# Query weights loaded and used ahead of the down weights, and 256 KB of the down weights dealt to 48 and 16 partitions, in a one-core decode step

## The chip, the core and the metric

The kernel runs on one core of a Trainium2 chip. A core has TensorE (PE; its weight loads are shown as PEld), VectorE (DVE), ScalarE (ACT), GpSimd (POOL), SyncE (SP, which here issues almost all transfers), and sixteen DMA engines that move data between HBM and the core's memory. The metric is the device time of one execution in microseconds (us); less is better. Before the change the median of three runs is 199.74 us (199.58 to 199.85).

## The reference

One decode step of a block: sliding-window attention over a cache, gated by a gated linear unit, for a batch of 8 rows and one new token each (D = 512).

```python
x = A_x                                    # [8, 1, 512] bf16
xn = _layernorm(x, axis=-1)
# A: 32 query heads, 8 K/V heads, head size 128, the last W = 2048 of 8192 cache rows
q = (xn @ wq) ...                          # wq [512, 4096]
scores = einsum("bhqd,bhkd->bhqk", q, k) * 128 ** -0.5
o = einsum("bhqk,bhkd->bhqd", softmax(scores), v)
s = o.reshape(8, 1, 4096) @ wo             # wo [4096, 512]
# B: F = 1792
h = sigmoid(xn @ w_gate) * (xn @ w_up)     # [512, 1792] each
g = silu(h @ w_down)                       # w_down [1792, 512]
return x + s * g
```

All inputs are bf16. The K and V windows are 33.5 MB each, the weights 14 MB.

## The kernel before, in words

**Transfers.** SP issues them in an order written out as a list, `todo`. `later` (L107) appends a tile's load with its pool's name; `pump` (L110) issues from the head of the list as long as the pool of the head has `room` (5 tiles of 16 KB per partition for "k", 4 for "v"); `free` (L116) gives a place back at the point of the program where a tile has been used, and pumps again. The instruction then waits on the chip until the place is really free. The order on SP's queue is the order of the list:

1. `x_bf` and the second half of the gate weights (L149, L151); ACT's queue loads the first half and `x4_sb` (L157)
2. `wu_sb`, the up weights, all rows
3. `wd_sb`, the down weights (L194): of the 14 rows of 512 that each of 128 partitions owns, rows 1 to 13
4. `wq_sb`, the query weights, in two tiles of 2 MB (L196)
5. `wd_part` (`want_part`, L179): the 128 rows left over, one per partition as `wd_sb` counts, dealt into another tile
6. sixteen K tiles and sixteen V tiles of 2 MB each (L202, L204), and `wo_sb` in five pieces (L206)

**The dealt rows.** `wd_part` is a tile of 64 partitions by 3 rows, cleared by a POOL memset (L183), and filled by three transfers (`PARTS`, L175 and L176): 20 partitions by 3 rows, again 20 by 3, and 8 by 1. `p0, n` are the partitions, `s0` the first of the rows, and `a` (5, 5, 4) is the outermost count on the HBM side; the inner piece is one row of 1 KB. Since rows in `wd_part` sit in other partitions than the values of the hidden layer that multiply them, three small matmuls (L327) with selection matrices `sel_part` (L276 to L285, a memset and seven DVE copies out of an identity) bring those values there, and a DVE copy makes `hP_sb` (L335).

**The first stage.** PE runs its instructions in program order: the gate and up products (`hidden`, L291), `hP_ps`, the 16 down products `w_ps` (L348: 13 from `wd_sb`, 3 from `wd_part`), the regrouping `b_ps` (L361), then the 32 query products `q_ps` (L385) and their transposes (L404), and then the attention, which starts with transposes of K (L481). ACT and DVE copy between (`w_sb` L358, `sigb` L371, `gg_sb` L375, `q_bf` L399 and L401, `qm_sb` L407).

**The attention.** For each of 8 batch rows two K tiles are transposed in parts of 8 (L481, DVE copies L486), multiplied with the queries (`scores`, L493), and two rows later in the loop the V tiles are multiplied (`values`, L591). PE, DVE and ACT interleave three batch rows. A used K or V tile calls `free`, which issues the next load.

**The end.** The output weights come in rows 0 to 12, 12 to 20, 20 to 26, 26 to 30 and 30 to 32. The first twenty products go to `part_ps` (L719), the last twelve to `fin_ps` (L733), each as its piece lands; then `prod` (L748), `y_bf` (L750) and the output transfer (L751).

Of the kernel before, what the change touches and what calls it, by code (L numbers as in the profile page):

```python
# [10 lines left out]
def kernel(  # L11
# [13 lines left out]
    nc = tc.nc  # L25
    P = 128
    B, _, D = A_x.shape
    _, Hkv, Sk, Dh = A_k_cache.shape
# [5 lines left out]
    FT = F // P  # L34
# [14 lines left out]
    bf16 = mybir.dt.bfloat16  # L49
    f32 = mybir.dt.float32  # L50
    AF = mybir.ActivationFunctionType
    ALU = mybir.AluOpType
# [6 lines left out]
    vpool = ctx.enter_context(tc.tile_pool(name="vpool", bufs=4))  # L59
    ktpool = ctx.enter_context(tc.tile_pool(name="ktpool", bufs=3))  # L60
    ppool = ctx.enter_context(tc.tile_pool(name="ppool", bufs=2))
    consts = ctx.enter_context(tc.tile_pool(name="consts", bufs=1))
    work = ctx.enter_context(tc.tile_pool(name="work", bufs=1))
    small = ctx.enter_context(tc.tile_pool(name="small", bufs=2))
    ps_t = ctx.enter_context(
        tc.tile_pool(name="ps_t", bufs=4, space=bass.MemoryType.PSUM)
    )
    ps_s = ctx.enter_context(
        tc.tile_pool(name="ps_s", bufs=2, space=bass.MemoryType.PSUM)
    )  # L70
# [3 lines left out]
    ps_m = ctx.enter_context(  # L74
        tc.tile_pool(name="ps_m", bufs=1, space=bass.MemoryType.PSUM)
    )
    ctx.enter_context(tc.manual_schedule())


# [1 line left out]
    q0, q1 = nc.sync, nc.scalar  # L81
    k_tiles = {}
    v_tiles = {}
    room = {"k": 5, "v": 4}
    pools = {"k": kpool, "v": vpool}

    def load_cache(cache, tag, b, i):
# [16 lines left out]
    weights = {}  # L104
    todo = []

    def later(tag, f):  # L107
        todo.append((tag, f))
# [7 lines left out]
    def free(tag):  # L116
        room[tag] += 1
        pump()

    def want_rows(name, w, tag, per, r0, r1):  # L120
        def f():
            t = load_rows(w, tag, per, r0, r1, name)
            for r in range(r0, r1):
                weights[(name, r)] = t[:, r - r0, :]

        later(tag, f)
# [13 lines left out]
    Z = 32  # L140
    S = Z // B
    NB = D // P
# [24 lines left out]

    A = 5  # L170
    SD = 1
    SX = 3
    HP = P // 2
    NA = 4 * A
    PARTS = ((0, NA, 0, SX, 0, A), (Z, NA, 0, SX, SX * NA, A))  # L175
    PARTS += ((Z + NA, P - 2 * SX * NA, 0, 1, 2 * SX * NA, 4),)  # L176
    d_room = []

    def want_part(w, per):  # L179
        def f():  # L180
            d = vpool.tile([HP, SX, SD, w.shape[1]], bf16, name="wd_part", tag="v")
            d_room.append(d)
            nc.gpsimd.memset(d[:], 0.0)  # L183
            for p0, n, x0, x1, s0, a in PARTS:
                m = n * (x1 - x0)
                src = w.rearrange("(y r) n -> y (r n)", r=per)[s0 : s0 + m]
                q0.dma_start(
                    out=d[p0 : p0 + n, x0:x1].rearrange("p x r n -> p (x r n)"),
                    in_=src.rearrange("(y a) n -> a y n", a=a)[:, :, : SD * w.shape[1]],
                )  # L190

        later("v", f)

    want_rows("wd_sb", B_w_down, "v", FT, SD, FT)  # L194
    for i in range(2):
        want_rows("wq_sb", A_wq, "k", KT, 2 * i, 2 * i + 2)  # L196
    want_part(B_w_down, FT)
    order = [(b, i) for b in range(B) for i in range(NQ)]
    AHEAD = 3
# [5 lines left out]
    for t0, t1 in ((0, 12), (12, KS), (KS, 26), (26, 30), (30, RT)):  # L205
# [4 lines left out]
    ident = consts.tile([P, P], bf16, name="ident")  # L210
# [6 lines left out]
        out=perm[:].rearrange("k (l p) -> k l p", l=G),  # L217
        in_=ident[:].rearrange("k (p l) -> k l p", l=G),
# [13 lines left out]
        out=rstd[:], in_=mv[:, 1:2], func=AF.Sqrt, bias=eps_t[:], scale=1.0  # L232
# [4 lines left out]
        out=xn_bf[:],  # L237
        in0=x_f[:],
# [7 lines left out]
    for kt in range(KT):  # L246
        nc.tensor.transpose(  # L247
            out=xnT_ps[:, kt, :],
            in_=xn_bf[:].rearrange("b (p kt) -> b kt p", kt=KT)[:, kt, :],
# [11 lines left out]
    for t in p_buf:  # L261
        nc.vector.memzero(t[:])
    oP_sb = work.tile([P, RT, Z], bf16, name="oP_sb")
    nc.vector.memzero(oP_sb[:])

    NDQ = Dh // RT
    own_q = consts.tile([P, NDQ], f32, name="own_q")
    nc.vector.reduce_sum(
        out=own_q[:], in_=ident_f[:].rearrange("k (h q) -> k q h", q=NDQ), axis=AX.X
    )  # L270
    sel_z = consts.tile([P, Z], f32, name="sel_z")
    nc.vector.reduce_sum(
        out=sel_z[:], in_=ident_f[:].rearrange("k (j z) -> k z j", z=Z), axis=AX.X
    )

    sel_part = consts.tile([P, SX, HP], bf16, name="sel_part")  # L276
    nc.vector.memzero(sel_part[:])
    for p0, n, x0, x1, s0, a in PARTS:
        for x in range(x0, x1):
            nc.vector.tensor_copy(  # L280
                out=sel_part[:, x, p0 : p0 + n].rearrange("k (a e) -> k a e", a=a),
                in_=ident[:, s0 : s0 + n * (x1 - x0)].rearrange(
                    "k (e x a) -> k x a e", x=x1 - x0, a=a
                )[:, x - x0],
            )  # L285

    FC = F // NB

    def hidden(name):  # L291
# [21 lines left out]
        out=h_sb[:].rearrange("k t p -> k p t"),  # L313
        in0=sig[:, :FC].rearrange("k (p t) -> k p t", t=FT),
        in1=u_ps[:].rearrange("k (p t) -> k p t", t=FT),
        op=ALU.mult,
    )
    free("v")
    hT_sb = work.tile([P, FT, Z], bf16, name="hT_sb")
    nc.vector.transpose(  # L320
        out=hT_sb[:].rearrange("k t z -> k (t z)"),
        in_=h_sb[:].rearrange("k t p -> k (t p)"),
    )

    hP_ps = ps_t.tile([HP, SX, SD * Z], f32, name="hP_ps", tag="t")
    for x in range(SX):
        nc.tensor.matmul(  # L327
            hP_ps[:, x, :],
            lhsT=sel_part[:, x, :],
            rhs=hT_sb[:, :SD, :].rearrange("p t z -> p (t z)"),  # L330
            start=True,
            stop=True,
        )
    hP_sb = work.tile([HP, SX, SD * Z], bf16, name="hP_sb")
    nc.vector.tensor_copy(out=hP_sb[:], in_=hP_ps[:])  # L335
    down = [(hT_sb[:, t, :], weights[("wd_sb", t)]) for t in range(SD, FT)]
    for x in range(SX):
        top = max(p0 + n for p0, n, x0, x1, _, _ in PARTS if x0 <= x < x1)
        down += [
            (hP_sb[:top, x, Z * r : Z * (r + 1)], d_room[0][:top, x, r, :])  # L340
            for r in range(SD)
        ]


    w_ps = ps_s.tile([P, D], f32, name="w_ps", tag="s")
    for t, (h, w) in enumerate(down):
        j = t % NB
        nc.tensor.matmul(  # L348
            w_ps[Z * j : Z * (j + 1), :],
            lhsT=h,  # L350
            rhs=w,
            start=(t < NB),
            stop=(t >= len(down) - NB),
            tile_position=(0, Z * j),
            skip_group_check=True,
        )
    w_sb = ktpool.tile([P, 2, 512], f32, name="w_sb", tag="kT")
    nc.scalar.copy(out=w_sb[:, 0], in_=w_ps[:])  # L358
    b_ps = ps_s.tile([P, P], f32, name="b_ps", tag="s")
    for j in range(NB):  # L360
        nc.tensor.matmul(  # L361
            b_ps[Z * j : Z * (j + 1), :],
            lhsT=sel_z[:],
            rhs=w_sb[:, 0, j * P : (j + 1) * P],
            start=True,
            stop=True,
            tile_position=(0, Z * j),
            skip_group_check=True,
        )
    sigb = work.tile([P, P], f32, name="sigb")  # L370
    nc.scalar.activation(out=sigb[:], in_=b_ps[:], func=AF.Sigmoid)  # L371
    free("v")
    free("v")
    gg_sb = work.tile([P, P], f32, name="gg_sb")
    nc.vector.tensor_tensor(out=gg_sb[:], in0=sigb[:], in1=b_ps[:], op=ALU.mult)  # L375

    JQ = NB
    q_ps = [ps_s.tile([P, rep * Dh], f32, name="q_ps", tag="s") for _ in range(2)]  # L380
    for kt in range(KT):
        for x in range(Hkv // JQ):
            for j in range(JQ):
# [3 lines left out]
                    lhsT=xnT_sb[:, kt, :],  # L387
                    rhs=weights[("wq_sb", kt)][:, g * rep * Dh : (g + 1) * rep * Dh],
                    start=(kt == 0),
                    stop=(kt == KT - 1),  # L390
                    tile_position=(0, Z * j),
                    skip_group_check=True,
# [3 lines left out]
    for x in range(Hkv // JQ):  # L396
        src = q_ps[x][:].rearrange("k (r d) -> k r d", r=rep)
# [4 lines left out]
    for x in range(Hkv // JQ):  # L402
        for r in range(rep):
            nc.tensor.transpose(  # L404
                out=qT_ps[:, x, r, :], in_=q_bf[:, x, r, :], identity=ident[:]
            )
        nc.vector.tensor_copy(  # L407
            out=qm_sb[:, :, x * JQ : (x + 1) * JQ, M0 : M0 + rep],
            in_=qT_ps[:, x].rearrange("d r (j z) -> d z j r", z=Z)[:, ::S],
# [2 lines left out]
    free("k")  # L412
    free("k")

    Hh = G * rep
    turn_rows = consts.tile([P, P], bf16, name="turn_rows")
# [2 lines left out]
    for i in range(NQ):  # L421
        nc.vector.tensor_copy(
            out=turn_rows[:].rearrange("k (i j l r) -> k i j l r", i=NQ, j=NJ, l=G)[
                :, i
            ],
            in_=ident[:].rearrange("k (l j i r) -> k i j l r", i=NQ, j=NJ, l=G)[:, i],
        )
        nc.vector.reduce_sum(
            out=sel_den[:, i * Hh : (i + 1) * Hh].rearrange("k (l r) -> k l r", l=G),
            in_=ident_f[:].rearrange("k (l j i r) -> k i l r j", l=G, j=NJ, i=NQ)[:, i],  # L430
            axis=AX.X,
        )
    for e in range(2):
        nc.vector.reduce_sum(
            out=sel_out[:, e, :].rearrange("k (i h) -> k i h", i=NQ),
            in_=ident_f[:].rearrange(
                "k (i m e h) -> k e i h m", i=NQ, m=NJ // 2, e=2
            )[:, e],
# [9 lines left out]
        out=sel_res[:],  # L448
        in0=sel_out[:, 0, :].unsqueeze(2).to_broadcast([P, Hq, NDQ]),
        in1=sel_out[:, 1, :].unsqueeze(2).to_broadcast([P, Hq, NDQ]),  # L450
        op=ALU.add,
# [333 lines left out]
```

## Time and profile before

| | |
|---|---|
| median of 3 runs | 199.74 us (199.58 to 199.85) |
| the profiled execution | 199.72 us, span 198.0 us |
| PE busy | 152.7 us (77% of the span) |
| DVE busy | 122.2 us (62%) |
| ACT busy | 37.6 us (19%) |
| POOL busy | 3.0 us (1%) |
| read from HBM | 81.02 MB, 409 GB/s over the span |
| K tile, from issue to landing | 30.3 us (median of 16) |
| V tile, from issue to landing | 27.1 us (median of 16) |
| PE waits for `wd_part` | 8.1 us, once |
| first K transpose | 34.2 us |

The span runs from the first to the last instruction of the profiled execution. Busy time counts the union of an engine's instructions. A transfer's time from issue to landing holds its wait behind the transfers issued before it. Beside the page, the trace keeps a record of each DMA packet (start, duration, bytes, queue; not its DMA engine) and the time of each semaphore increment.

### The profile page before, as it was taken

How to read it: one execution, taken by the hardware profiler on the slowest of the kernel's cores; microseconds unless marked ns; L12 is line 12 of the kernel's file. 1: busy time of each engine (PE TensorE's matmuls, PEld its weight loads, DVE VectorE, ACT ScalarE, POOL GpSimd, SP SyncE). 2: the span in 40 equal slices, each digit the busy share in tenths (PEclk: the TensorE clock that was granted, in tenths of full speed). 3: DMA queues.
4: the chain of work that ended last, by engine and by line, in shares of the span. 5: the costliest groups of instructions: out<-in, count | busy, mean ns of one | idle time of the engine just before them, and what ended most of it. 6: DMA issues, size and time to landing. Idle time of an engine off the chain costs nothing.

```text
span 198.0 us, 4772 instructions
## 1 busy us (share of the span) xinstructions
PE 152.7 (77%) x2133; PEld 103.3 (52%) x2133; DVE 122.2 (62%) x234; ACT 37.6 (19%) x91; POOL 3.0 (1%) x11
## 2 busy tenths in 40 slices
PE   0434038799979999989798969996989797898552
PEld 0111014677666677656565646674657565566421
DVE  3764002999978679758675937687858674852301
ACT  3200011000720610240024000600140033082010
POOL 5000000000000000000000000000000000000000
PEclk9999999999999999999999969999999999999975
DMA  6999999999999999999999999999999999999980
GB/s 207 433 438 428 428 443 427 434 424 422 430 427 434 427 434 427 427 430 427 427 427 435 427 430 430 422 434 424 430 427 434 427 434 430 427 424 422 421 341 10
DMA packets 6441, 81.32 MB, mean 411 GB/s; under 512 B 782, under 2 KB 918, under 8 KB 1558
## 3 DMA queue, kind: packets, MB, share of 16 engines
q1 hardware_dynamic: 6242, 80.10, 95.0%
q10 hardware_dynamic: 180, 0.93, 1.4%
q8 instruction: 16, 0.26, 0.5%
q14 instruction: 3, 0.02, 0.0%
HBM read 81.02 MB, written 0.01 MB: 409 GB/s over the span
## 4 chain that ended last, share of the span: by engine, by line
DMA 57%; PE 34%; ACT 3%; DVE 3%; SPq 1%; issue 1%
DMA k_sb<-in_A_k_cache_dram 33%; PE kT_ps L481 17%; DMA wo_sb<-in_A_wo_dram 11%; DMA wd_part<-in_B_w_down_dram 10%; PE o_ps L597 6%; PE s_ps L500 5%; DMA wg_sb<-in_B_w_gate_dram 3%; ACT p_buf L548 2%; PE pT_ps L571 2%; PE q_ps L385 1%; DVE kT_sb L486 1%; SPq L99 1%; ACT L548 1%; PE fin_ps L733 1%; PE qT_ps L404 0%
## 5 line engine op out<-in xcount | busy, mean ns | idle before, releaser
L486 DVE COPY kT_sb<-kT_ps 128x1024 bf16<-128x1024 bf16 x128 | 85.1, 686 | 30.8 <-PE kT_ps L481 30.1
L481 PE MATMUL kT_ps<-perm,k_sb 128*128 128x128 bf16 x1024 | 75.8, 221 | 10.1 <-DMA k_sb<-in_A_k_cache_dram 10.1
L481 PEld LDWEIGHTS <-k_sb 128*128 128x128 bf16 x1024 | 59.1, 99 | 29.8 <-issue 16.2
L597 PE MATMUL o_ps<-v_sb,pT_sb 128*32 128x256 bf16 x512 | 39.7, 276 | 1.6 <-DVE o_sb L618 0.9
L500 PE MATMUL s_ps<-kT_sb,qm_sb 128*32 128x512 bf16 x256 | 25.8, 393 | 1.9 <-DVE kT_sb L486 1.9
L597 PEld LDWEIGHTS <-pT_sb 128*32 128x32 bf16 x512 | 21.9, 96 | 10.2 <-issue 3.5
L548 ACT ACTIVATE p_buf<-s_ps,nb 32x512 bf16<-32x512 f32 x32 | 21.7, 678 | 0.5
L541 ACT COPY nb<-m_ps 128x1 f32<-128x1 f32 x8 | 1.3, 159 | 87.0 <-PE m_ps L535 87.0
L571 PE MATMUL pT_ps<-turn_rows,p_buf 128*128 128x128 bf16 x128 | 10.9, 230 | 1.5 <-ACT p_buf L548 1.5
L564 DVE COPY pT_sb<-pT_ps 128x1024 bf16<-128x1024 bf16 x14 | 9.6, 687 | 3.9 <-PE pT_ps L571 3.9
L500 PEld LDWEIGHTS <-qm_sb 128*32 128x32 bf16 x256 | 6.7, 93 | 8.8 <-issue 2.4
L571 PEld LDWEIGHTS <-p_buf 128*128 128x128 bf16 x128 | 9.3, 150 | 3.4 <-ACT p_buf L548 2.1
L613 ACT ACTIVATE o_odd<-o_ps,own_col 128x128 f32<-128x128 f32 x8 | 2.9, 368 | 28.5 <-PE o_ps L597 28.4
L375 DVE TENSOR_TENSOR gg_sb<-sigb,b_ps 128x128 f32<-128x128 f32 x1 | 0.3, 289 | 12.0 <-ACT sigb L371 12.0
L348 PE MATMUL w_ps<-wd_part,hP_sb 52*32 52x512 bf16 (+1 forms) x3 | 0.6, 597 | 8.1 <-DMA wd_part<-in_B_w_down_dram 8.1
L548 ACT ACTIVATION_READ_ACCUMULATOR p_buf<-s_ps,nb 32x1 f32 x32 | 5.9, 184 | 0.0
L515 DVE TENSOR_REDUCE st<-s_ps 128x1 f32<-128x512 f32 x8 | 5.5, 681 | 0.5 <-PE s_ps L500 0.5
L618 DVE SCALAR_TENSOR_TENSOR o_sb<-o_ps,own_col,o_odd 128x128 f32<-128x128 f32 x8 | 2.7, 339 | 3.5 <-ACT o_odd L613 3.5
L348 PEld LDWEIGHTS <-hP_sb 52*32 52x32 bf16 (+1 forms) x3 | 0.1, 97 | 9.0 <-issue 9.0
L640 DVE SCALAR_TENSOR_TENSOR own<-m_ps,inv,own_q 128x128 f32<-128x128 f32 x8 | 2.8, 346 | 3.1 <-PE m_ps L631 3.1
L247 PE MATMUL xnT_ps<-ident,xn_bf 8*128 8x8 bf16 x4 | 0.3, 174 | 5.4 <-DVE xn_bf L236 5.4
L295 PEld LDWEIGHTS <-xnT_sb 128*32 128x32 bf16 x32 | 1.1, 119 | 6.3 <-issue 5.8
(80 smaller groups left out, 67.9 us busy)
## 6 DMA issues: line engine op xcount, KB each, us to landing
k_sb<-in_A_k_cache_dram SPq DMA_DIRECT2D x16, 2048.0 KB, 30.3
v_sb<-in_A_v_cache_dram SPq DMA_DIRECT2D x16, 2048.0 KB, 27.1
wq_sb<-in_A_wq_dram SPq DMA_DIRECT2D x2, 2048.0 KB, 20.2
wu_sb<-in_B_w_up_dram SPq DMA_DIRECT2D x1, 1792.0 KB, 10.4
wd_sb<-in_B_w_down_dram SPq DMA_DIRECT2D x1, 1664.0 KB, 13.9
wo_sb<-in_A_wo_dram SPq DMA_DIRECT2D x1, 1536.0 KB
wo_sb<-in_A_wo_dram SPq DMA_DIRECT2D x1, 1024.0 KB, 20.4
wg_sb<-in_B_w_gate_dram ACTq DMA_DIRECT2D x1, 896.0 KB
```

The source lines that it names most:

```text
L99: q0.dma_start(out=t[:], in_=w.rearrange("(p r) n -> p r n", r=per)[:, r0:r1, :])
L481: nc.tensor.transpose(out=kT_ps[:, c, :], in_=k_sb[:, j * CU + h * CH + c, :], identity=perm[:],)
L486: nc.vector.tensor_copy(out=kT[(b, u)][:, h * CH : (h + 1) * CH, :], in_=kT_ps[:])
L500: nc.tensor.matmul(s_ps[b][NR * l : NR * (l + 1), :], lhsT=qm_sb[:, b, i * G + l, o : o + Z], rhs=t[:, :, PG * l : PG * (l + 1)], start=(u ...
L515: nc.vector.reduce_max(out=st[b][:], in_=s_ps[b][:], axis=AX.X)
L548: nc.scalar.activation(out=p_buf[b % 2][rows, :, l, :], in_=s[rows, :].rearrange("k (c p) -> k p c", p=PG), func=AF.Exp, bias=nb[rows, :], ...
L564: copy(out=pT[b][:, h * CH : (h + 1) * CH, :], in_=pT_ps.pop(h)[:])
L571: nc.tensor.transpose(out=pT_ps[h][:, c, :], in_=p_buf[b % 2][:, :, :, h * CH + c].rearrange("k p l -> k (p l)"), identity=turn_rows[:],)
L597: nc.tensor.matmul(o_ps[rows, b % 2, :].rearrange("k (e d) -> k e d", e=2), lhsT=pT[b][:, c, rows], rhs=v[:, m, c], start=(c == 0), stop=( ...
L613: nc.scalar.mul(out=o_odd[:], in_=o_ps[:, b % 2, Dh:], mul=own_col[:, 1:2])
L618: nc.vector.scalar_tensor_tensor(out=o_of[b // 2][:, b % 2, :], in0=o_ps[:, b % 2, :Dh], scalar=own_col[:, 0:1], in1=o_odd[:], op0=ALU.mul ...
L640: nc.vector.scalar_tensor_tensor(out=own[:], in0=m_ps[:, b % 2, P : 2 * P].rearrange("p (q t) -> p q t", q=NDQ), scalar=inv[y][:, b % 2 : ...
```

## The change

The query weights move ahead of the down weights in SP's list, and the query products, with their casts and transposes, move ahead of `hP_ps` and the down products in the program. Of the down weights `wd_sb` now holds rows 2 to 13 of every partition (12 rows). The other 256 rows go to two tiles of a pool of their own, `d_pool`: 48 partitions (`a` = 6) and 16 partitions (`a` = 2), by 2 by 2 rows, one transfer each, with an inner piece of two rows (2 KB). They are full, so no memset clears them. Each has its selection matrix (one DVE copy), two selection matmuls and one cast, and four down products each, so that there are 20 in place of 16. The "v" pool holds one tile less in this stage.

```diff
+    d_pool = ctx.enter_context(tc.tile_pool(name="d_pool", bufs=1))
...
-    room = {"k": 5, "v": 4}
+    room = {"k": 5, "v": 4, "d": 1}
...
-    A = 5
-    SD = 1
-    SX = 3
-    HP = P // 2
-    NA = 4 * A
-    PARTS = ((0, NA, 0, SX, 0, A), (Z, NA, 0, SX, SX * NA, A))
-    PARTS += ((Z + NA, P - 2 * SX * NA, 0, 1, 2 * SX * NA, 4),)
+    SD = 2
+    PE = P // 16
+    SHARES = ((6, 0), (2, 6 * PE * SD))
     d_room = []
 
     def want_part(w, per):
         def f():
-            d = vpool.tile([HP, SX, SD, w.shape[1]], bf16, name="wd_part", tag="v")
-            d_room.append(d)
-            nc.gpsimd.memset(d[:], 0.0)
-            for p0, n, x0, x1, s0, a in PARTS:
-                m = n * (x1 - x0)
-                src = w.rearrange("(y r) n -> y (r n)", r=per)[s0 : s0 + m]
+            for a, s0 in SHARES:
+                n = a * PE
+                t = d_pool.tile([n, SD, SD, w.shape[1]], bf16, name=f"wd_part{a}")
+                src = w.rearrange("(y r) n -> y (r n)", r=per)[s0 : s0 + n * SD]
                 q0.dma_start(
-                    out=d[p0 : p0 + n, x0:x1].rearrange("p x r n -> p (x r n)"),
-                    in_=src.rearrange("(y a) n -> a y n", a=a)[:, :, : SD * w.shape[1]],
+                    out=t[:].rearrange("p u r n -> p u (r n)"),
+                    in_=src.rearrange("(y a) n -> a y n", a=a)[
+                        :, :, : SD * w.shape[1]
+                    ],
                 )
-        later("v", f)
-
-    want_rows("wd_sb", B_w_down, "v", FT, SD, FT)
+                d_room.append((t, n, a, s0))
+
+        later("d", f)
+
     for i in range(2):
         want_rows("wq_sb", A_wq, "k", KT, 2 * i, 2 * i + 2)
+    want_rows("wd_sb", B_w_down, "v", FT, SD, FT)
     want_part(B_w_down, FT)
...
+    sel_part = []
+    for _, n, a, s0 in d_room:
+        sel = consts.tile([P, SD, n], bf16, name=f"sel_part{n}")
+        nc.vector.tensor_copy(
+            out=sel[:].rearrange("k u (a p) -> k u a p", a=a),
+            in_=ident[:, s0 : s0 + n * SD].rearrange(
+                "k (p u a) -> k u a p", u=SD, a=a
+            ),
+        )
+        sel_part.append(sel)
...
+    # behind the query products, their transposes and the two free("k")
+    down = [(hT_sb[:, t, :], weights[("wd_sb", t)]) for t in range(SD, FT)]
+    for (d, n, a, s0), sel in zip(d_room, sel_part):
+        ps = ps_t.tile([n, SD, SD * Z], f32, name="hP_ps", tag="t")
+        for u in range(SD):
+            nc.tensor.matmul(
+                ps[:, u, :],
+                lhsT=sel[:, u, :],
+                rhs=hT_sb[:, :SD, :].rearrange("p t z -> p (t z)"),
+                start=(u == 0),
+                stop=True,
+                skip_group_check=True,
+            )
+        hP_sb = work.tile([n, SD, SD * Z], bf16, name=f"hP_sb{n}")
+        nc.vector.tensor_copy(out=hP_sb[:], in_=ps[:])
+        down += [
+            (hP_sb[:, u, Z * r : Z * (r + 1)], d[:, u, r, :])
+            for u in range(SD)
+            for r in range(SD)
+        ]
```

The selection matrices of before (L276 to L285), the three selection matmuls and the list of down products at their old place (L325 to L342) go; the products `w_ps` to `gg_sb` (L345 to L375) follow the new list unchanged, with one `free("v")` instead of two.

More of the change, by code (lines that the diff above doesn't have):

```diff
@@ L274 @@
     )
[L276 to L285, printed above, removed]
     FC = F // NB
@@ L323 @@
     )
[L325 to L375, printed above, removed]
     JQ = NB
@@ L413 @@
     free("k")
+    down = [(hT_sb[:, t, :], weights[("wd_sb", t)]) for t in range(SD, FT)]
[17 more added lines that the diff above has]
+        ]
+    w_ps = ps_s.tile([P, D], f32, name="w_ps", tag="s")
+    for t, (h, w) in enumerate(down):
+        j = t % NB
+        nc.tensor.matmul(
+            w_ps[Z * j : Z * (j + 1), :],
+            lhsT=h,
+            rhs=w,
+            start=(t < NB),
+            stop=(t >= len(down) - NB),
+            tile_position=(0, Z * j),
+            skip_group_check=True,
+        )
+    w_sb = ktpool.tile([P, 2, 512], f32, name="w_sb", tag="kT")
+    nc.scalar.copy(out=w_sb[:, 0], in_=w_ps[:])
+    b_ps = ps_s.tile([P, P], f32, name="b_ps", tag="s")
+    for j in range(NB):
+        nc.tensor.matmul(
+            b_ps[Z * j : Z * (j + 1), :],
+            lhsT=sel_z[:],
+            rhs=w_sb[:, 0, j * P : (j + 1) * P],
+            start=True,
+            stop=True,
+            tile_position=(0, Z * j),
+            skip_group_check=True,
+        )
+    sigb = work.tile([P, P], f32, name="sigb")
+    nc.scalar.activation(out=sigb[:], in_=b_ps[:], func=AF.Sigmoid)
+    free("v")
+    gg_sb = work.tile([P, P], f32, name="gg_sb")
+    nc.vector.tensor_tensor(out=gg_sb[:], in0=sigb[:], in1=b_ps[:], op=ALU.mult)
     Hh = G * rep
```

## The prediction, made before the result was known

> **What bounds the kernel now.** I read the slices of the page first, then the DMA queues, then windows over the end, then the timeline of the last operations, and last the trace's own DMA records.
>
> ```profile
> DMA  6999999999999999999999999999999999999980
> GB/s 207 433 438 428 428 443 427 434 424 422 430 427 434 427 434 427 427 430 427 427 427 435 427 430 430 422 434 424 430 427 434 427 434 430 427 424 422 421 341 10
> ...
> q1 hardware_dynamic: 6242, 80.10, 95.0%
> ...
> q8 instruction: 16, 0.26, 0.5%
> q14 instruction: 3, 0.02, 0.0%
> ```
>
> The transfers run at full share from the second slice to the 38th. In the third part, q1 is SP's queue. q8 and q14 fetch the engines' instructions, and travel on the same 16 DMA engines.
>
> ```profile
> 27.00:190.00 163.00, 143.43 (x2017) 99.44 (x2017) 111.07 (x207) 33.63 (x86) 0.00 (x0) 0.99 1.01 429
> 190.00:191.00 1.00, 0.65 (x8) 0.12 (x7) 0.00 (x0) 0.00 (x0) 0.00 (x0) 0.73 0.86 352
> 191.00:192.00 1.00, 0.33 (x4) 0.00 (x0) 0.00 (x0) 0.58 (x1) 0.00 (x0) 0.50 0.70 285
> 192.00:193.00 1.00, 0.99 (x32) 0.93 (x33) 0.00 (x0) 0.00 (x0) 0.00 (x0) 0.50 0.58 229
> 193.00:194.00 1.00, 0.88 (x28) 0.54 (x21) 0.00 (x0) 0.00 (x0) 0.00 (x0) 0.50 0.12 43
> ```
>
> In these windows the last two columns are DMA share and GB/s. The share is 1 up to 190 us and then falls in steps to 0.12: the DMA engines finish one after another over some 3.5 us, and the last one ends the kernel:
>
> ```profile
> 193.42 1.00 PE L733 MATMUL fin_ps<-wo_sb,oP_sb 128*32 128x128 bf16 x24
> ...
> 194.47 0.29 DVE L748 TENSOR_TENSOR prod<-gg_sb,fin_ps 128x128 f32<-128x128 f32 x1 [6.13 <-PE fin_ps L733]
> 194.79 0.29 DVE L750 TENSOR_TENSOR y_bf<-prod,x_sb 128x128 bf16<-128x128 f32 x1
> 195.11 0.64 SPq L751 DMA_DIRECT2D out_dram<-y_bf  x1
> ```
>
> The chain of waits names PE for 34%, but each transfer on it was issued 20 to 30 us before it landed, behind others. PE's lateness is no bound.
>
> So each DMA engine's own load matters. The trace has a record for every packet (start, duration, bytes, queue) and for each increment of a semaphore; a full-width transfer gives sixteen. The last piece of `wo_sb` landed on the sixteen engines, in us after 190.51:
>
> ```
> 0  .16  .61  1.04  1.17  1.28  2.10  2.82  2.86  2.90  2.96  2.99  3.04  3.05  3.33  3.46
> ```
>
> An engine's packets follow one another without a gap (16 KB start every 607 ns), so it can be followed from transfer to transfer. Each then keeps its lag, except where it carries a fetch. In all:
>
> - Eight engines ("H") fetch 16 KB for PE twice each. A 16 KB fetch puts the engine 1.42 us back. They end at 2.86 to 3.46.
> - Five, A to E, carried `wd_part`; their lags after it were 1.11, 1.20, 1.22, 1.36, 1.62. B carried two 8 KB fetches (0.84 each; DVE's by their distance of 126 of its instructions) and ends at 2.82. E carried one (0.55) and ends at 2.10. A, C, D end at 1.04, 1.17, 1.28.
> - Three had neither and end at 0, .16, .61.
>
> [...]
>
> **The change, part by part.**
>
> *Twelve `w_down` rows for thirteen on all partitions.* A 13 KB packet took 498 ns and a 12 KB one 460, both overlapping the next by 4; eight on each engine: −0.30 us for all sixteen.
>
> *The dealt rows before.* The three transfers of `wd_part` gave 6, 6 and 5 increments, of which one came at issue: they ran on 5, 5 and 4 engines, the 5, 5 and 4 of the outer count `a`. The four of the third are among the five. A, B, D, E moved 26 packets of 1 KB (24.673 to 25.792 us for A, so 1.12 us), and C 24 (1.03).
>
> *The dealt rows after.* `a` is 6 and 2, so 96 pieces of 2 KB on 6 engines, then 32 on 2: sixteen pieces an engine in each. [...]
>
> The nearest row for 2 KB pieces is the last of `wo_sb`, eight an engine in 0.643 us. So 1.29 us on six engines and 2.57 on two of them. The bounds for the 32 pieces are 2.43 (at the rate of 14 KB packets, 531 ns each) and 2.74 (at 42.8 ns per KB of `wd_part`). I take 2.57, from a row of the same piece size.
>
> Net per engine: the two, −.30 −1.12 +2.57 = **+1.15**. Others of A, B, D, E −.14; C −.05; the sixth +.98 (from at most .61, harmless); the H engines −.30, so at most 3.46 − .30 = 3.16.
>
> *Which two?* The smaller sets lay in the larger ones, also with the 4 engines that loaded `x4_sb`: they are A, B, D, E. So the two are of these four. The H engines are hit in a fixed order, twice round; the lags they had before `wd_part` were, in that order, .11 .27 .07 .17 .20 .26 .72 .53. The others had E .52, B .09, D .25, A 0 / C .20 / .01, .25, .70. If both halves have the same pattern, one rotation alone gives four, one and three that fit: .53 .11 .27 .07 / .17 / .20 .26 .72. It starts with E's twin and B's. So I take **E and B**.
>
> *At the end:* E 2.10 + 1.15 = 3.25; B 2.82 + 1.15 = 3.97; H 3.16. The last landing goes from 3.46 to 3.97, **+0.51 us** (+0.37 to +0.68 with the bounds above). Everything behind it (eight matmuls, two DVE steps, the output transfer) follows by the same.
>
> *Query weights first.* SP issues `wq_sb` (0.46 to 0.55 us each) before `wd_sb` (0.70), one small transfer fewer, and the order on its queue costs nothing: it issues by 9.2 us what the engines are busy with to 25 us. The `wq_sb` tiles land at 16.9 and 21.8 instead of 20.9 and 25.7. PE's 32 `q_ps` matmuls (28.65 to 32.8) move into the 8.1 us in which PE waited for `wd_part`; ACT's cast (.58) and DVE's (.69, and two copies of .29) go with them. The small transfers land later, at 26.8 + 1.15 = 27.9, and behind it wait 8 `w_ps` matmuls (.6), `w_sb` (.59), `b_ps` (.65), so PE is through at about 30.1. The K transposes are queued behind these, but the first K tile lands at 32.6 (31.5 before, +1.15). They start then, not at 34.2: 1.6 us earlier, and worth nothing, because K and V tiles come at 4.86 us each whatever PE does. Were that cover gone, the late `wd_part` would cost its 1.15.
>
> *Instructions.* Two `hP_ps`-like groups (4 matmuls for 3), 20 `w_ps` matmuls for 16 at some .11 each, one more cast (.25) on DVE, six copies and a memset fewer (7 took .73, the memset .14): all in the wait for `wd_part` or for K. POOL's memset (1.38) goes; behind it `ident` and x's normalisation start up to .6 earlier, and then wait for the gate weights (7.8). PE has five matmuls more; the last fetch came at matmul 2029 of 2133, the next would at about 2150, so no fetch is added.
>
> *Slots.* `v` has one tile less to hold, so the first V transfer waits for one release less; the queue never ran dry, so nothing.
>
> The sum: this execution took 199.72 us (span 198.0 and 1.7 around it), 0.02 under the median. 199.72 + 0.51 = **200.23 us**.
>
> **The rivals.**
>
> 1. *The pair misses B.* Then B gets one share only and ends at 2.82 − .14 = 2.68. With E in the pair the last landing is 3.25: −0.21, 199.51; with A and D it is H's 3.16: −0.30, 199.42. This is the case on the other side. It decides when B's lag stays under 3.46 − 1.15 = 2.31, or B's share is one. For it: a packet record carries no engine number, so B's place rests on the likeness of two patterns. Against: of eight rotations one fits.
> 2. *The transfers spread over all sixteen*, so that the dealing does nothing: each carries 8 pieces, .64 − .30 on the H engines: +0.34, 200.06. Against it: the increments 6, 6, 5.
> 3. *PE is the bound*, as the chain's 34% suggests. Then the 1.6 us that K transposes gain are the kernel's: 198.1. Against it: DMA share 1.01 from 27 to 190 us.
> 4. *A landing slows more than its sum*, as when one more 8 KB fetch falls on B before the end: .84 more, 201.1. Against it: DVE has five instructions fewer.
>
> **How the numbers follow.** Forecast case (B and E): 0.80, with 200.0 to 200.5 as its own range (+0.37 to +0.68, and some 0.1 from run to run: the three runs of before lie 0.27 apart). Rival 1: 0.14. Rivals 2, 3, 4: 0.02 each. A range of 199.5 to 200.5 takes in the forecast, rival 2 and about half of rival 1. The bound of a measurement is 0.2%, 0.40 us. Of the forecast case 0.82 lies above it: slower 0.80 × 0.82 + 0.02 (rival 4) = 0.68. Within: the rest of it, 0.14, rival 1 nearly whole, 0.13, and rival 2: 0.29. Faster: rival 3 and a tail of 1: 0.03.
>
> **What would show it right or wrong.** In the profile after: `w_down`'s two small transfers give 7 and 3 increments, 6 and 2 of them with data; the share in the windows at the end falls earlier for fourteen engines and stays at a low tail for one (a sixteenth, 0.06) for some 0.8 us; `prod` starts at about 195.0 instead of 194.47; the K transposes start at about 32.6. I am wrong if the tail shortens (another pair), if sixteen increments land, if the fetches move to other engines, or if K's first landing stays at 31.5.

## The result, and the profile after

The change made the kernel slower, by three times what was forecast: 201.18 us median (200.85 to 201.47, 6 runs) against 199.68 us (199.55 to 199.85, 6 runs), a ratio of 1.0074 with a 95% interval of 1.0064 to 1.0085. The profiled execution took 201.29 us (span 199.5), 1.57 more than that of before.

The slices of the changed kernel, DMA share and GB/s:

```profile
DMA  6999999999999999999999999999999999999980
GB/s 210 434 450 424 416 313 427 450 420 427 422 427 440 417 440 424 427 434 427 430 430 422 430 437 427 422 430 427 437 417 437 430 427 430 424 430 425 417 331 11
```

The share is as full as before, but the sixth slice, 25 to 30 us, moved 313 GB/s where its neighbours have 416 and 427. The engines were busy and moved less. The same stretch in windows (the last two columns are DMA share and GB/s), before:

```profile
25.00:27.00 2.00, 0.07 (x3) 0.10 (x3) 0.00 (x0) 0.00 (x0) 0.00 (x0) 1.00 0.98 408
27.00:30.00 3.00, 2.03 (x22) 0.71 (x24) 0.29 (x1) 0.86 (x2) 0.00 (x0) 1.00 1.02 437
```

and after:

```profile
25.00:27.00 2.00, 1.82 (x16) 0.87 (x19) 0.81 (x4) 0.00 (x0) 0.00 (x0) 1.00 1.04 259
27.00:30.00 3.00, 1.37 (x16) 0.37 (x8) 0.00 (x0) 0.00 (x0) 0.00 (x0) 1.00 0.97 350
```

This is when the dealt pieces move. In the packet records they run from 24.45 to 28.79 us; the first take 84 ns, from 25.0 us on up to 201 (median 120), and the 16 KB packets of the first K tile beside them, on engines that carry no dealt piece too, grow from 611 ns to as much as 1098.

The windows over the end of the changed kernel:

```profile
191.00:192.00 1.00, 0.00 (x0) 0.00 (x0) 0.00 (x0) 0.00 (x0) 0.00 (x0) 1.00 0.93 387
192.00:193.00 1.00, 0.61 (x8) 0.12 (x7) 0.00 (x0) 0.31 (x1) 0.00 (x0) 0.97 0.77 313
193.00:194.00 1.00, 0.67 (x16) 0.47 (x20) 0.00 (x0) 0.28 (x1) 0.00 (x0) 0.50 0.69 279
194.00:195.00 1.00, 0.71 (x24) 0.51 (x20) 0.00 (x0) 0.00 (x0) 0.00 (x0) 0.50 0.28 107
195.00:196.00 1.00, 0.86 (x24) 0.55 (x23) 0.00 (x0) 0.00 (x0) 0.00 (x0) 0.50 0.03 12
```

A share of 0.03 in the last microsecond is a single engine (one of sixteen is 0.06) for half of it. The timeline behind it:

```profile
195.12 1.05 PE L725 MATMUL fin_ps<-wo_sb,oP_sb 128*32 128x128 bf16 x24 [0.41 <-DMA wo_sb<-in_A_wo_dram]
...
196.21 0.29 DVE L740 TENSOR_TENSOR prod<-gg_sb,fin_ps 128x128 f32<-128x128 f32 x1 [6.23 <-PE fin_ps L725]
196.53 0.29 DVE L742 TENSOR_TENSOR y_bf<-prod,x_sb 128x128 bf16<-128x128 f32 x1
196.86 0.66 SPq L743 DMA_DIRECT2D out_dram<-y_bf  x1
```

`prod` starts 1.74 us later than before (194.47). The last piece of `wo_sb` landed on the sixteen engines, in us after the first of them, which was at 190.51 before and at 191.50 after:

```
before  0  .16  .61 1.04 1.17 1.28 2.10 2.82 2.86 2.90 2.96 2.99 3.04 3.05 3.33 3.46
after   0  .12  .75 1.34 1.94 2.81 2.86 2.92 2.92 3.07 3.15 3.22 3.54 3.60 3.97 4.22
```

So the last landing moved by 1.75 us in two parts: 0.99 for the first engine, and with it for all, and 0.76 more of lag (how far an engine ends behind the first) for the last. The first engine carries no dealt piece and one row less, and should have gained 0.30. It lost 1.33 between the end of `wd_sb` and that of the first K tile (24.36 to 30.55 us, 6.19 for 4.86): that is the slow stretch. The last engine stood 1.40 behind after the first K tile and carried two of PE's instruction fetches later (1.42 each): 4.22.

### The profile page after: what moved, and what is told of

Same layout as the page of the kernel before. It is cut to its first block, busy times and chain, and to the rows that moved or that the text cites. A ratio compares the mean times of both kernels' runs of the same rounds, so it can differ in the third digit from the quotient of the medians.

```text
span 199.5 us, 4772 instructions
## 1 busy us (share of the span) xinstructions
PE 155.9 (78%) x2138; PEld 105.4 (53%) x2138; DVE 122.5 (61%) x229; ACT 37.6 (19%) x91; POOL 1.4 (1%) x10
## 4 chain that ended last, share of the span: by engine, by line
DMA 76%; PE 21%; SPq 1%; issue 0%; DVE 0%
DMA k_sb<-in_A_k_cache_dram 61%; PE kT_ps L473 13%; DMA wo_sb<-in_A_wo_dram 11%; PE o_ps L589 4%; DMA wg_sb<-in_B_w_gate_dram 3%; PE s_ps L492 3%; SPq L100 1%; PE fin_ps L725 1%; PE pT_ps L563 0%; SPq L150 0%; DVE prod L740 0%; PE m_ps L527 0%; DVE y_bf L742 0%; PE m_ps L510 0%; SPq L90 0%
## 5 line engine op out<-in xcount | busy, mean ns | idle before, releaser
L473 PE MATMUL kT_ps<-perm,k_sb 128*128 128x128 bf16 x1024 | 77.9, 225 | 13.4 <-DMA k_sb<-in_A_k_cache_dram 13.4
L473 PEld LDWEIGHTS <-k_sb 128*128 128x128 bf16 x1024 | 61.1, 101 | 33.8 <-issue 16.4
L327 PE MATMUL q_ps<-wq_sb,xnT_sb 128*32 128x512 bf16 x32 | 3.8, 626 | 6.2 <-DMA wq_sb<-in_A_wq_dram 6.2
L327 PEld LDWEIGHTS <-xnT_sb 128*32 128x32 bf16 x32 | 1.3, 130 | 8.6 <-issue 8.6
L343 DVE CAST q_bf<-q_ps 128x512 bf16<-128x512 f32 x1 | 0.7, 692 | 7.1 <-PE q_ps L327 7.1
L291 PEld LDWEIGHTS <-xnT_sb 128*32 128x32 bf16 x32 | 1.1, 119 | 6.7 <-issue 6.2
```

The lines of the kernel that those rows point to most:

```text
L327: nc.tensor.matmul(q_ps[x][Z * j : Z * (j + 1), :], lhsT=xnT_sb[:, kt, :], rhs=weights[("wq_sb", kt)][:, g * rep * Dh : (g + 1) * rep * Dh ...
L473: nc.tensor.transpose(out=kT_ps[:, c, :], in_=k_sb[:, j * CU + h * CH + c, :], identity=perm[:],)
```

## The experiments

A share below is the sixteen 2 KB pieces that one transfer of the change gives an engine. In the table, "slow" counts the 16 KB data packets over 618 ns that start between 15 and 40 us, and gives what they took over 611 ns, added up and divided by the sixteen engines; an instruction fetch alone makes one of them (before: one, 0.03 us). "Pieces" are the dealt packets. "Last" is the last landing of `wo_sb` in the profiled execution.

| kernel | median, us | its before | ratio (95%) | pieces, ns (median, longest) | slow: count, us an engine | last |
|---|---|---|---|---|---|---|
| before | | | | 46, 46 | 1, 0.03 | 193.97 |
| after | 201.18 | 199.68 | 1.0074 (1.0064 to 1.0085) | 120, 201 | 79, 1.05 | 195.72 |
| e1_order_only | 199.43 | 199.49 | 0.9997 (0.9987 to 1.0006) | 46, 46 | 1, 0.03 | 193.65 |
| e2_deal_only | 201.26 | 199.49 | 1.0087 (1.0068 to 1.0106) | 121, 194 | 87, 0.99 | 195.41 |
| e3_four_each | 200.46 | 199.49 | 1.0044 (1.0029 to 1.0058) | 84, 84 | 1, 0.03 | 194.52 |
| e4_before_eight_each | 200.45 | 199.49 | 1.0057 (1.0018 to 1.0097) | 46, 101 | 36, 0.41 | 194.12 |
| e5_five_and_three | 199.65 | 199.70 | 1.0003 (0.9994 to 1.0012) | 84, 84 | 1, 0.03 | 193.74 |
| e6_no_dealing | 200.04 | 199.70 | 1.0023 (1.0014 to 1.0032) | none | 2, 0.03 | 194.08 |
| e7_shifted_by_four | 199.93 | 199.70 | 1.0012 (1.0003 to 1.0021) | 46, 92 | 4, 0.10 | 194.23 |
| e8_upper_half | 200.36 | 199.50 | 1.0050 (1.0032 to 1.0068) | 55, 102 | 60, 0.85 | 194.65 |

The first four experiments and e8 ran on one chip, e5 to e7 on another. Each has runs of the kernel before beside it, so times are compared by their distance from these; e1 takes the same time as the kernel before, so its profile can stand for that kernel's on the chip of e1 to e4.

The theory after this profile, 'destination' in what was expected, was that the slow stretch comes from where the pieces are written. The increments with data say that a transfer ran on as many engines as its `a` counts (5, 5 and 4 before, 6 and 2 after). If each count is one engine, the dealing of before gave each of its five engines four consecutive partitions from 0 on and four more from 32 on, and that of after gives eight consecutive ones; a packet record names neither engine nor partition. The eight pieces of the third transfer of before, two on each of four engines (partitions 52 to 59), took 46 ns like the others. The rivals were the order of the loads ('order'), and the reading of 2 KB pieces with gaps ('piece').

**e1, the order alone.** The loads (`want_rows`) and the products are moved as in the change; the dealing stays as it was.

```diff
-    want_rows("wd_sb", B_w_down, "v", FT, SD, FT)
     for i in range(2):
         want_rows("wq_sb", A_wq, "k", KT, 2 * i, 2 * i + 2)
+    want_rows("wd_sb", B_w_down, "v", FT, SD, FT)
     want_part(B_w_down, FT)
... (the products move too)
```

> The old dealing (1 KB pieces, four partitions an engine) in the new order: query weights loaded and used first. In the changed kernel 16 KB packets took up to 1.05 us instead of 0.61 between 25 and 29.4 us, and the engine that finishes first lost 1.0 us. [...] Theory 'order' (the small transfers now follow the down weights): slow packets, about 201.2 us.

No slow packet but the one beside a fetch, and no difference in time. Its window:

```profile
25.00:27.00 2.00, 2.00 (x20) 0.75 (x17) 0.52 (x2) 0.00 (x0) 0.00 (x0) 1.00 1.08 451
```

The order alone is worth nothing and costs nothing.

**e2, the dealing alone.** The changed kernel with the loads and the products in the old order.

```diff
+    want_rows("wd_sb", B_w_down, "v", FT, SD, FT)
     for i in range(2):
         want_rows("wq_sb", A_wq, "k", KT, 2 * i, 2 * i + 2)
-    want_rows("wd_sb", B_w_down, "v", FT, SD, FT)
     want_part(B_w_down, FT)
... (the products move too)
```

> The new dealing in the old order of loads and of products. 'Destination' and 'piece': slow packets around 25 to 30 us and about 201.2 us, all of the change's loss. 'Order': no slow packets; the lags alone give 199.5 to 200.2.

The whole loss is there, with the slow stretch:

```profile
25.00:27.00 2.00, 0.00 (x0) 0.00 (x0) 0.00 (x0) 0.00 (x0) 0.00 (x0) 1.00 1.05 288
```

**e3, the same pieces in other partitions.** The source, the sizes and the count of engines stay; each share is split in two transfers.

```diff
-                n = a * PE
+                m = 4 * a
+                n = Z + m
                 t = d_pool.tile([n, SD, SD, w.shape[1]], bf16, name=f"wd_part{a}")
-                src = w.rearrange("(y r) n -> y (r n)", r=per)[s0 : s0 + n * SD]
-                q0.dma_start(
-                    out=t[:].rearrange("p u r n -> p u (r n)"),
...
+                nc.gpsimd.memset(t[:], 0.0)
+                for z in range(2):
+                    y0 = s0 + z * m * SD
+                    src = w.rearrange("(y r) n -> y (r n)", r=per)[y0 : y0 + m * SD]
+                    q0.dma_start(
+                        out=t[Z * z : Z * z + m].rearrange("p u r n -> p u (r n)"),
... (the selection matrices follow)
```

> The changed kernel with the same 2 KB pieces on the same engines, but each engine's pieces go to four partitions at 4e and four at 32+4e (partitions 0 to 23 and 32 to 55, and 0 to 7 and 32 to 39) in place of eight consecutive ones; a memset clears the gap. 'Destination': no slow packets, the last landing follows from the lags alone, 199.5 us or a little less than before. 'Piece' and 'order': as the changed kernel, 201.2.

```profile
25.00:27.00 2.00, 2.00 (x23) 0.64 (x20) 0.72 (x3) 0.00 (x0) 0.00 (x0) 1.00 1.07 448
27.00:30.00 3.00, 1.80 (x16) 0.36 (x16) 0.00 (x0) 0.86 (x2) 0.00 (x0) 1.00 1.02 438
```

The slow packets are gone: every piece took 84 ns, no 16 KB packet went over 618 but for one beside a fetch. So it is the destination, not the piece or the order; against e2, on the same chip, that is 0.80 us. But the time did not come down to 199.5. It kept 0.97 us of the loss, which the theory of the destination doesn't explain. The landings do. The lags after the first K tile are 2.9 and 3.0 for two engines (two shares) and 1.4, 1.5, 1.6, 1.7 for four (one share). Followed to the end, the one at 1.69 takes two fetches of PE (+1.43 and +1.41) and lands last, at 4.52; the next is at 3.46. Against e1's the last landing is 0.87 later (194.52 for 193.65), most of the 0.97. Five of the six are A to E; the sixth engine, dealt to for the first time, is one that fetches for PE.

**e4, the kernel before with eight partitions an engine.** The converse: the 1 KB pieces of before, to consecutive partitions.

```diff
-    PARTS = ((0, NA, 0, SX, 0, A), (Z, NA, 0, SX, SX * NA, A))
-    PARTS += ((Z + NA, P - 2 * SX * NA, 0, 1, 2 * SX * NA, 4),)
+    PARTS = ((0, 2 * NA, 0, SX, 0, A),)
+    PARTS += ((2 * NA, P - 2 * SX * NA, 0, 1, 2 * SX * NA, 4),)
```

> The kernel before, with its 1 KB pieces dealt to 40 consecutive partitions (eight an engine) by one transfer, and the eight rows left over to 8 more. 'Destination': slow packets, for about half as long as in the changed kernel since half as many bytes are dealt: 200.2 to 200.8 us. 'Piece' and 'order': 199.7.

```profile
25.00:27.00 2.00, 0.00 (x0) 0.00 (x0) 0.00 (x0) 0.00 (x0) 0.00 (x0) 1.00 1.06 354
```

A slow stretch appears in a kernel that had none, with the old pieces and the old order. The runs of this kernel scatter from 199.68 to 203.2 us, four of ten over 202.5. The ratio leaves out the two longest; without these the median is 199.93. The profile is of the fastest, 0.19 above the median of before, so what the others lose is not shown by it: e4 shows the slow stretch, but not its price.

**e5, the sixth engine spared.** e3 with the same bytes on five engines (16 pieces each) and on three of them (16 more).

```diff
-    SHARES = ((6, 0), (2, 6 * PE * SD))
+    SHARES = ((5, 0), (3, 5 * PE * SD))
... (and the edit of e3)
```

> The run with four partitions at a time (e3) had no slow packets and still took 1.0 us more than the kernel before: its last engine carried one share of the dealt rows and two of PE's instruction fetches. Here the same 256 KB in the same 2 KB pieces go to five engines (16 pieces each) and to three of these (16 more), so that the sixth has none. Theory 'sixth engine fetches': this is 0.5 to 1.2 us faster than e3. Where the engine with DVE's two fetches is not among the three, the last landing is 3.2 us after the first engine's of the kernel before, 0.2 less than there, 199.3 us; where it is, 3.97, or 200.0 us. Theory 'it is the bytes dealt, whichever engine has them': as e3, 200.4.

It stands 0.05 us under its runs of before where e3 stood 0.97 over its own, 1.02 us less, and the last landing went from 194.52 to 193.74. The engine with the two 8 KB fetches has a single share here (1.56 after the first K tile, +0.84 and +0.85 later), the one with the single such fetch a double (2.93 + 0.55), the other two doubles have no fetch. So the first three are E and two of A, C, D (A and D, if C is the fifth, as the prediction took it), and B is not among them. The forecast for that case was 0.2 us better than before; the last landing is 0.23 earlier than in the profile of before, and the time is the same within its interval. It beats neither kernel by what could be told apart.

**e6, no dealing at all.** All 14 rows on all partitions, in one transfer.

```diff
-    want_rows("wd_sb", B_w_down, "v", FT, SD, FT)
+    want_rows("wd_sb", B_w_down, "v", FT, 0, FT)
...
-    want_part(B_w_down, FT)
```

> The kernel before without any dealing: all 14 rows of the down weights on all 128 partitions in one transfer, no selection matmuls, no memset. Theory 'each DMA engine's own load sets the end': the engines that fetch for PE get 8 KB more, 0.30 us, and the last landing comes 0.3 us later, 199.8 us, while five engines end 0.8 us earlier. Theory 'one pipe, only the bytes in all count': 199.5 us, or a little less for the three small transfers that go.

0.34 us slower, where the sum of one engine's load said 0.30. The profiled execution was the shortest of the ten, and its last landing is only 0.11 later than in the profile of before. The eight engines that fetch for PE now end last, at 2.8 to 3.4 us after the first; seven of the other eight end within 0.8 us of the first. So it is each engine's own load that counts, not the bytes in all.

**e7, moved up by four partitions.** The runs so far leave open whether it takes eight consecutive partitions an engine, or which partitions they are. Here the pieces of before go, four partitions an engine, to 4 to 23, 36 to 55 and 56 to 63.

```diff
-    PARTS = ((0, NA, 0, SX, 0, A), (Z, NA, 0, SX, SX * NA, A))
-    PARTS += ((Z + NA, P - 2 * SX * NA, 0, 1, 2 * SX * NA, 4),)
+    PARTS = ((4, NA, 0, SX, 0, A), (Z + 4, NA, 0, SX, SX * NA, A))
+    PARTS += ((Z + NA + 4, P - 2 * SX * NA, 0, 1, 2 * SX * NA, 4),)
```

> [...] Theory 'eight partitions an engine': no slow packets, 199.5 us.

```profile
25.00:27.00 2.00, 0.00 (x0) 0.00 (x0) 0.00 (x0) 0.00 (x0) 0.00 (x0) 1.00 1.05 423
```

A miss as it was put: there are slow packets, but four, one of them beside a fetch, and a loss of 0.1%. Other partitions than those of before cost little here, and the next run moves the pieces further.

**e8, in the upper half.** The same four partitions an engine, at 64 to 83, 96 to 115 and 116 to 123.

```diff
-    PARTS = ((0, NA, 0, SX, 0, A), (Z, NA, 0, SX, SX * NA, A))
-    PARTS += ((Z + NA, P - 2 * SX * NA, 0, 1, 2 * SX * NA, 4),)
+    PARTS = ((HP, NA, 0, SX, 0, A), (HP + Z, NA, 0, SX, SX * NA, A))
+    PARTS += ((HP + Z + NA, P - 2 * SX * NA, 0, 1, 2 * SX * NA, 4),)
... (the tile, its memset and the selection matrix grow from 64 to 128 partitions)
```

> [...] Theory 'eight consecutive partitions an engine is what slows': no more slow packets than in the kernel before; 199.6 us.

```profile
25.00:27.00 2.00, 0.00 (x0) 0.00 (x0) 0.00 (x0) 0.00 (x0) 0.00 (x0) 1.00 1.07 286
27.00:30.00 3.00, 0.62 (x3) 0.14 (x3) 0.00 (x0) 0.55 (x1) 0.00 (x0) 1.00 0.97 396
```

60 slow packets and 0.86 us more time, with four partitions an engine, and with the pieces, the order and the three transfers of before. So where the pieces are written is the cause, and not the count of partitions an engine writes alone. What makes one place dear (e2, e4, e8) and another cheap (before, e3, e7) no run shows. And e8 differs from e7 in the half of the partitions, where the slow runs in the lower half (e2, e4) dealt eight partitions an engine, not four.

## Why the prediction was wrong, point by point

The direction was right; the time lay outside the range. Two terms failed. The first is the price of the 2 KB pieces, which took no account of where they are written and put nothing for the engines beside them: the first engine alone lost 1.33 us there. The second is the sixth engine, whose +.98 was called harmless, and which ended last, at 4.22. In e3 only the second was left.

- **What bounds the kernel**, each DMA engine's own load: right. e6 gave +0.34 for a forecast 0.30, and the landings of e3 and e5 are the sums of shares and fetches. In the changed kernel it holds outside the slow stretch only.
- **Twelve rows for thirteen, −0.30 on all**: right in size (the packets took 460 ns).
- **The 2 KB pieces, 0.643 us for eight**: right in e3 (the first and the second half land 0.65 apart on the last of the six). In the changed kernel the term failed: the dealt pieces ran until 28.79 us, 4.3 us from the first to the last, where e3 has 2.8 and the term for 32 pieces was 2.57, with bounds of 2.43 and 2.74. Those were taken from rows of other transfers, in which the packets of a size took nearly the same time (before: every 2 KB packet 84 ns, every dealt 1 KB packet 46, the 14 KB ones 535 to 545). The destination of the new tiles, 8 partitions for each engine where there were 4 and 4, was in the diff and was not priced.
- **The other engines untouched**: wrong, and it was not even put as a term. All sixteen lost, the first 1.33 us. Together with the slowed pieces this is the 0.80 us between e2 and e3.
- **Which two engines**: half right. E is one: it lags by 3.41 after the first K tile of the changed kernel and ends at 3.97, with .55 for its fetch. B is not, so the part of rival 1 that concerns the pair came true. The likeness of two patterns of lags misled: B has one share in e5, so it is not among the first three. Even the rotation that was taken set .20 against a lag of .01.
- **"The sixth +.98 (from at most .61, harmless)"**: the step that failed in the lags. The sixth was taken for one of the three engines without fetches. It is one of the eight that fetch for PE: 1.4 us (1.7 in e3) after its share, and 2.83 on top: 4.22, where the forecast's last lag was 3.97. Alone (e3) this made 0.97 us, and with the sixth engine spared (e5) the loss was gone. The 0.51 forecast for B came from a like sum on another engine, so its nearness to a part of the result is chance.
- **Query weights first, worth nothing**: right, e1 at 0.9997 (0.9987 to 1.0006). The K transposes did not start at 32.6 as said but at 34.51, since the first K tile landed at 34.46; the cover over `wd_part` held (PE was through with `b_ps` at 31.9):

```profile
29.92 0.61 PE L381 MATMUL w_ps<-wd_part,hP_sb 16*32 16x512 bf16 x4 [1.54 <-DMA wd_part<-in_B_w_down_dram]
31.22 0.65 PE L394 MATMUL b_ps<-w_sb,sel_z 128*32 128x128 f32 x8 [0.69 <-ACT w_sb L391]
34.51 2.74 PE L473 MATMUL kT_ps<-perm,k_sb 128*128 128x128 bf16 x24 [2.63 <-DMA k_sb<-in_A_k_cache_dram]
```

- **No fetch added**: right, sixteen of PE and three of 8 KB, as before.
- **The rivals.** 2 was excluded (7 and 3 increments, as foreseen), 3 as well. Rival 4, more than the sum, was nearest to what happened, by another mechanism than the one it named, and it had 0.02.

## What to carry to other kernels

Where transfers fill all DMA engines, cost a change on each engine by itself: what it moves, what else rides on it (instruction fetches here), and where it writes. The same 2 KB pieces cost 0.80 us less of the kernel's time with four and four partitions an engine (e3) than with eight consecutive ones (e2), and where they were slowed, engines that dealt nothing were too (the first lost 1.33 us). Which destination is cheap was told here by runs and their packet records alone. Before an engine is given more, find out what it carries already: one run that spares it shows it more surely than a pattern in the lags.

## What the runs showed of the hardware that was not expected

- With the pieces at eight consecutive partitions an engine all sixteen engines slowed: in the changed kernel 16 KB packets took up to 1098 ns for 611 (1019 and 1025 on the first engine, which dealt nothing), and the core's rate fell from 420 GB/s (20 to 25 us) to 259 (25 to 27 us). How the slowness spreads from the dealt pieces to the engines that deal nothing no run here shows.
- Another place can cost little or much: 0.10 us an engine in e7 against 0.85 in e8, with the same bytes and the same four partitions an engine. What differs in the transfers is the partitions, moved up by four or into the upper half.
- A 16 KB instruction fetch puts the engine that carries it 1.41 to 1.43 us back, where 16 KB of data take 0.61 (before: a fetch of 924 ns, and the data packet beside it 1115 for 611). The sixteen fetches of PE in the kernel before went round eight engines, twice, and the changed kernel has sixteen again.
